# Attention inputs loaded in six pieces a tensor in place of four, and the longest rows of the first loads halved

## The chip, the core and the metric

The kernel runs on one core of a Trainium2 chip. The metric is the device time of one execution in microseconds (us); lower is better. Three executions of the kernel before took 612.52, 612.87 and 614.18 us, so its time is 612.87 us, the median.

## What is computed

Windowed attention, and then a mixture of experts on its output. Cut to what matters:

```python
batch, n_heads, seq, head_dim = (8, 8, 576, 64)
scores = scale * np.matmul(q, k.transpose(0, 1, 3, 2))
rel = pos[:, None] - pos[None, :]
mask = (rel >= 0) & (rel < window)                  # window = 64
scores = np.where(mask, scores, -1000000000.0)
attn = np.exp(scores - np.max(scores, axis=-1, keepdims=True))
attn = attn / (np.sum(attn, axis=-1, keepdims=True) + 1e-09)
attn_out = np.matmul(attn, v)
x = attn_out.transpose(0, 2, 1, 3).reshape(B * S, H * D)   # 4608 x 512
logits = x @ w_gate                                  # 8 experts, 576 tokens each
# tokens are given to experts in the order of their logits, each once, up to a capacity
h = np.maximum(x[mask] @ w1[e], 0.0)
out[mask] = h @ w2[e]
```

## The kernel before

**Stages.** The attention takes the first 147 us or so of the program. Then the tokens are routed, and from about 160 us on eight experts run one after another, with weights streamed in and the results scattered out. The change touches the attention's loads alone.

**The attention.** The queries of one batch are cut into 9 blocks of 64 positions (NB = 9). A step `m` of the loop at L291 works on two blocks, so 8 batches make 36 steps and a new batch begins every four and a half. On TensorE (PE) a step is: the scores of step `m` (L128, tiles Q and K), where a batch begins or goes on also its gate products (L85, tile VT, the values once more, transposed) and their transposes (L95), the product with the values of step `m - 2` (L178, tiles VO and VE), and the transposes of step `m - 1` (L148). ScalarE (ACT) takes the exponentials, VectorE (DVE) the masks, maxima and scalings, GpSimd (POOL) copies values by half a block (VE, L114 and L115). The order is the one that is written; each engine runs its own part in that order and waits on semaphores.

**The loads.** All come from the queue of SyncE (SP), but for two pieces of K at the very start, which ACT issues. For the first two batches, `load_qk`, `load_vt` and `load_v` (L57 to L75) are called with ranges of blocks (L235 to L253); a row is what one of the 128 partitions gets in one DMA, and so it has 1,024 to 5,120 bytes there, cut out of a longer row in memory. From the third batch on `load_all` (L255) loads Q and K in one step and VT and VO in the next, each in four pieces that lie in memory one behind another; a piece has 128 rows of 576 numbers (2,304 bytes) for Q, K and VT, and of 584 (2,336 bytes) for VO. A rest of VO (64 rows of 2,336 bytes, L269) follows. The host writes that order in `lay` (L421). So a batch from the third on takes 17 DMAs. Outputs of the attention go out as stores `xs<-x` (L285) on the same queue, at first held back (HOLD = 14) and let go when the last loads have been issued.

**What limits the queue.** The DMAs of SP share eight semaphores in turn, DMAHW0 to DMAHW7. A DMA waits for the one eight places before it, so at most eight are on their way.

Of the kernel before, what the change touches and what calls it, by code (L numbers as in the profile page):

```python
# [20 lines left out]
B, H, S, D = 8, 8, 576, 64  # L21
NB = S // 64
HP = H // 2
E = 8
WARM = 30
VW = 73
# [2 lines left out]
LOADED = 9 * (B - 3) + 12  # L29


def attention(ctx, tc, c, q, k, v, vt, gate, xs, L, choices, setup, counters, mean, rows, guess):

    nc = tc.nc
    wgbd, wg = gate
# [6 lines left out]
    x = ps.tile([128, 512], FT, name="Tp", bufs=2)  # L42
# [8 lines left out]
    Q, K, VO, VE, VT = {}, {}, {}, {}, {}  # L51
# [2 lines left out]
    PARTS = ((0, 4), (4, NB))  # L54
    BW = HP * 64

    def load_vt(b, i0, i1):  # L57
        if not i0:
            VT[b] = ld.tile([128, NB, HP, 64], FT, name="VT")
        nc.sync.dma_start(VT[b][:, i0:i1].rearrange("p i h s -> p (i h s)"), vt[b, :, BW * i0:BW * i1])  # L60

    def load_qk(b, i0, i1, q2=nc.sync):
        if not i0:
            Q[b] = ld.tile([128, NB, HP, 64], FT, name="Q", bufs=3)
            K[b] = ld.tile([128, NB, HP, 64], FT, name="K", bufs=3)
        for q1, t, x in ((nc.sync, Q, q), (q2, K, k)):
            q1.dma_start(t[b][:, i0:i1].rearrange("p i h s -> p (i h s)"), x[b, :, BW * i0:BW * i1])

    def load_v(b, i0, i1):
        if not i0:  # L70
            VO[b] = ld.tile([128, 5, H, VW], FT, name="VO", bufs=3)
        j0, j1 = i0 // 2, i1 // 2
        nc.sync.dma_start(VO[b][:, j0:j1].rearrange("p j h w -> p (j h w)"), v[b, :, H * VW * j0:H * VW * j1])
        if i1 % 2:
            nc.sync.dma_start(VO[b][0:64, j1].rearrange("p h w -> p (h w)"), v[b, 0:64, H * VW * j1:])  # L75

# [148 lines left out]
    def last():  # L225

        for g, pe in enumerate(P.pop(M - 1)):
# [5 lines left out]
            T.setdefault(M - 1, []).append(pt)  # L233

    load_qk(0, 0, 2, nc.scalar)  # L235
    load_qk(0, 2, 4, nc.scalar)
    nc.sync.dma_start(wgbd, wg)
    counters()
    load_vt(0, *PARTS[0])
    load_qk(0, 4, 6)  # L240
    load_v(0, *PARTS[0])
    load_qk(0, 6, 8)
    load_vt(0, *PARTS[1])
    load_v(0, *PARTS[1])
    load_qk(0, 8, NB)
    load_qk(1, 0, 1)
    load_qk(1, 1, 3)
    load_vt(1, *PARTS[0])
    load_v(1, *PARTS[0])
    load_qk(1, 3, 5)  # L250
    load_qk(1, 5, NB)
# [3 lines left out]
    def load_all(b, part):  # L255
        if not part:
            Q[b] = ld.tile([128, NB, HP, 64], FT, name="Q", bufs=3)
            K[b] = ld.tile([128, NB, HP, 64], FT, name="K", bufs=3)
        else:
            VT[b] = ld.tile([128, NB, HP, 64], FT, name="VT")  # L260
            VO[b] = ld.tile([128, 5, H, VW], FT, name="VO", bufs=3)
        for t, x in ((VT[b], vt), (VO[b][:, 0:4], v)) if part else ((Q[b], q), (K[b], k)):
            t = t.rearrange("p i h w -> p (i h w)").rearrange("p (n x) -> p n x", n=4)
            n = 512 * t.shape[2]
            rows = x[b].rearrange("p x -> (p x)")[0:n].rearrange("(n p x) -> n p x", n=4, p=128)
            for i in range(4):
                nc.sync.dma_start(t[:, i], rows[i])
        if part:
            nc.sync.dma_start(VO[b][0:64, 4].rearrange("p h w -> p (h w)"),  # L269
                              v[b].rearrange("p x -> (p x)")[n:n + 64 * H * VW].rearrange("(p x) -> p x", p=64))  # L270
# [20 lines left out]
    for m in range(M + 1):  # L291
# [65 lines left out]
        for x in loads.get(m, []):  # L357
            load_all(*x)
# [56 lines left out]
def lay(q, k, v, wg):  # L415
    import numpy as np
    def blocks(t):
        t = t.reshape(B, HP, 2, NB, 64, D).transpose(0, 2, 5, 3, 1, 4)
        return np.ascontiguousarray(t).reshape(B, 128, NB * HP * 64)

    va = np.zeros((B, 640, H, VW), np.float32)  # L421
    va[:, :S, :, :D] = v.transpose(0, 2, 1, 3)
    va[:, :S, :, VW - 1] = 1.0
    va = np.ascontiguousarray(va.reshape(B, 5, 128, H * VW).transpose(0, 2, 1, 3)).reshape(B, 128, 5 * H * VW)

    def pieces(t, n):

        t[2:] = t[2:].reshape(B - 2, 128, n, -1).transpose(0, 2, 1, 3).reshape(B - 2, 128, -1)
        return t

    wb = np.zeros((128, HP, 32), np.float32)
    w = wg.reshape(HP, 2, D, E)
    wb[0:64, :, 0:8] = w[:, 0].transpose(1, 0, 2)
    wb[64:128, :, 16:24] = w[:, 1].transpose(1, 0, 2)
    return dict(q=pieces(blocks(q), 4), k=pieces(blocks(k), 4), v=pieces(va, 5), vt=pieces(blocks(v), 4), wg=wb)


NT = 4608
# [976 lines left out]
def body(tc, q, k, v, vt, wg, w1, w2, xs, out):  # L1415
    nc = tc.nc
    with ExitStack() as ctx:
# [6 lines left out]
        with ExitStack() as actx:  # L1424
            attention(actx, tc, c, q, k, v, vt, (wgs, wg), xs, L, lambda j0, j1: rt.choices(j0, j1, 0), rt.setup,
                      rt.counters, (rt.mean, rt.mean_mm, rt.mean_out), rt.rows, rt.guess)
# [49 lines left out]
```

## Time and profile before

| what | us |
|---|---|
| three executions, median | 612.87 (612.52 to 614.18) |
| the profiled execution, its own time | 613.34 |
| its span, first to last instruction | 611.7 |
| PE busy | 588.9 (96%) |
| DVE, ACT, POOL busy | 394.1, 371.8, 198.4 |
| DMA queue q1 (hardware), share of 16 engines' span | 36.0% |

The profile tells of one execution, of 613.34 us, from which 1.6 us lie outside its span. Busy shares are means over stages with different limits; the attention is read by itself below, in stretches of the span. A row of the timeline gives start, length, engine, line, operation, output and input, shape, and in brackets the idle time of the engine before it with what ended that. "issue" there means that the engine waited for nothing that the profile shows. The DMA view of a stretch lists queues with packets, megabytes and the share of 16 engines that their packets took; q1 carries the loads and stores that SP issues, q8 and q14 carry instructions.

### The profile page before, as it was taken

The numbers are of one execution on the slowest core, as the hardware profiler recorded it, in microseconds if no ns is written. First come the engines' busy times: TensorE is split into PE (matmuls) and PEld (weight loads), VectorE is DVE, ScalarE is ACT, GpSimd is POOL, SyncE is SP. The second block draws the span as 40 slices with busy tenths as digits, with TensorE's granted clock in tenths as the row PEclk, the third lists the DMA queues.
The fourth block names the chain that finished last, engine by engine and source line by source line (L and its number), as shares of the span: only waits on it lengthen the run. The fifth ranks groups of instructions, "written<-read, shape, count | busy, mean of one in ns | idle before, by whom it ended". The sixth has DMA issues, their size and how long they took to land.

```text
span 611.7 us, 15537 instructions
## 1 busy us (share of the span) xinstructions
PE 588.9 (96%) x5713; PEld 503.3 (82%) x5713; DVE 394.1 (64%) x1804; ACT 371.8 (61%) x804; POOL 198.4 (32%) x277
## 2 busy tenths in 40 slices
PE   7899999997699999999999999999999999999995
PEld 6677878886499789878988997898899789889984
DVE  6798988888785587369547936773685466705400
ACT  6799989997465477267537735852774375615410
POOL 1334435862431261054117203511530273011011
PEclk9999999998699999999999999999999999999999
DMA  8999999962698699189748938992895689410001
GB/s 314 362 359 358 362 365 376 384 240 89 183 242 173 247 210 243 43 289 229 152 167 229 245 70 270 216 221 97 257 243 111 233 191 330 169 44 34 2 26 53
DMA packets 46104, 128.87 MB, mean 211 GB/s; under 512 B 5824, under 2 KB 6464, under 8 KB 46016
## 3 DMA queue, kind: packets, MB, share of 16 engines
q1 hardware_dynamic: 31744, 79.00, 36.0%
q0 software_dynamic: 13984, 48.25, 34.1%
q8 instruction: 46, 0.75, 0.5%
q10 hardware_dynamic: 288, 0.52, 0.3%
q14 instruction: 42, 0.34, 0.2%
HBM read 82.14 MB, written 18.87 MB: 165 GB/s over the span
## 4 chain that ended last, share of the span: by engine, by line
PE 50%; issue 15%; DMA 5%; POOL 2%; DVE 1%; ACT 1%; POOLq 0%; SPq 0%
PE h L1328 23%; PE o L1372 20%; PE o L1362 4%; DMA st<-w 2%; DMA wl<-st 2%; POOL out L1351 2%; PE tp L1266 1%; DMA xg<-xs,idx 1%; PE rps L685 1%; PE rps L1046 1%; POOL xg L1228 0%; ACT wh L1155 0%; POOLq L1472 0%; POOL wl L1171 0%; DVE hl L1297 0%
## 5 line engine op out<-in xcount | busy, mean ns | idle before, releaser
L1328 PE MATMUL h<-xh,wh 128*128 128x320 f32 (+2 forms) x800 | 159.0, 333 | 0.3 <-DVE hh L1297 0.3
L1328 PEld LDWEIGHTS h<-xh,wh 128*128 128x128 f32 x800 | 124.2, 188 | 5.6 <-ACT sum L1287 0.5
L1351 POOL DMA_INDIRECT out<-ot,idx x40 | 40.1, 1001 | 198.1 <-DVE q L932 82.1
L1372 PE MATMUL o<-wh,hl 128*128 128x512 f32 x256 | 101.3, 396 | 0.0
L1372 PE MATMUL o<-wl,hh 128*128 128x512 f32 x256 | 100.5, 393 | 0.0
L1372 PE MATMUL o<-wh,hh 128*128 128x512 f32 x256 | 100.4, 392 | 0.0
L141 ACT ACTIVATE pe<-st,mx 128x128 f32<-128x128 f32 x288 | 92.0, 394 | 5.4 <-DVE mx L136 5.0
L1328 PE MATMUL h<-xh,wl 128*128 128x256 f32 (+1 forms) x512 | 91.1, 298 | 0.0
L1328 PEld LDWEIGHTS h<-xh,wl 128*128 128x128 f32 x512 | 78.5, 188 | 4.1
L1171 POOL DMA_DIRECT2D wl<-st x51 | 45.9, 1023 | 82.1 <-ACT wl L1169 43.8
L1155 ACT ACTIVATE wh<-st 128x1024 fp32r<-128x1024 f32 x64 | 67.3, 1051 | 4.9 <-DMA st<-w 4.7
L1342 ACT ACTIVATE ot<-o 128x512 f32<-128x512 f32 x32 | 19.2, 599 | 83.7 <-PE o L1372 83.7
L136 DVE CUSTOM_DVE_ANT_0 st<-Sp,mask 128x128 f32<-128x128 f32 x288 | 63.7, 285 | 5.9 <-PE Sp L128 4.5
L1372 PEld LDWEIGHTS o<-wl,hh 128*128 128x128 f32 x256 | 48.1, 188 | 9.5
L1372 PEld LDWEIGHTS o<-wh,hh 128*128 128x128 f32 x256 | 48.1, 188 | 9.4
L1372 PEld LDWEIGHTS o<-wh,hl 128*128 128x128 f32 x256 | 48.1, 188 | 9.3
L1169 ACT ACTIVATE wl<-wh 128x1024 fp32r<-128x1024 f32 x51 | 53.9, 1058 | 1.0
L1289 DVE TENSOR_TENSOR sum<-h,sum 128x256 f32<-128x256 f32 x56 | 23.4, 418 | 40.3 <-ACT sum L1287 39.7
L1292 ACT ACTIVATE hh<-h 128x320 fp32r<-128x320 f32 (+1 forms) x72 | 30.8, 427 | 30.2 <-PE h L1328 30.0
L1228 POOL DMA_INDIRECT xg<-xs,idx x32 | 32.4, 1012 | 42.2 <-DVE eq L970 34.6
L1297 DVE SCALAR_TENSOR_TENSOR hl<-h,hh 128x256 fp32r<-128x256 f32 x72 | 30.0, 417 | 24.1 <-ACT hh L1292 24.0
L153 ACT ACTIVATE pt<-Tp 128x512 f32<-128x512 f32 x70 | 41.1, 587 | 6.7 <-PE Tp L148 6.6
(222 smaller groups left out, 1028.4 us busy)
## 6 DMA issues: line engine op xcount, KB each, us to landing
st<-w SPq DMA_DIRECT2D x59, 512.0 KB, 7.6
wl<-st POOLq DMA_DIRECT2D x51, 512.0 KB, 8.6
xs<-x SPq DMA_DIRECT2D x36, 256.0 KB, 5.8
VO<-v SPq DMA_DIRECT2D x24, 292.0 KB, 6.4
Q<-q SPq DMA_DIRECT2D x24, 288.0 KB, 6.9
K<-k SPq DMA_DIRECT2D x24, 288.0 KB, 6.2
VT<-vt SPq DMA_DIRECT2D x24, 288.0 KB, 5.8
st<-w POOLq DMA_DIRECT2D x5, 512.0 KB, 7.9
```

The costliest lines, as they stand in the source:

```text
L136: nc.vector.tensor_tensor_reduce(st[:, h, :], Sp[h % 2][:, h // 2], mk, scale=-0.125, scalar=3.0e38, op0=OP.add, op1=OP.min, accum_out=mx[ ...
L141: nc.scalar.activation(pe[:, h, :], st[:, h, :], AF.Exp, bias=mx[:, h:h + 1], scale=-1.0)
L153: return pt, lambda: nc.scalar.activation(flat, Tp, AF.Copy)
L1155: nc.scalar.activation(hi, st[i], AF.Copy)
L1169: nc.scalar.activation(lo, hi.bitcast(FT), AF.Copy, scale=-1.0)
L1171: nc.gpsimd.dma_start(lo.bitcast(FT), st[i], accum_op=OP.add)
L1228: nc.gpsimd.indirect_dma_start(out=g[a][0:n], out_offset=None, in_=self.xs, in_offset=IndirectOffsetOnAxis(ap=idx[0:n, a:a + 1], axis=0))
L1292: nc.scalar.activation(hh[:, f, c0:c1], h, AF.Relu)
L1297: nc.vector.scalar_tensor_tensor(t, h[:, a - c0:b - c0], 0.0, hh[:, f, a:b].bitcast(FT), op0=OP.max, op1=OP.subtract)
L1328: nc.tensor.matmul(h[:, 0:w], wv[:, cc, 128 * (f % 2):128 * (f % 2) + 128], x[:, cc, x0:x0 + w], start=(k == 0), stop=(k == 4 * len(terms) ...
L1351: nc.gpsimd.indirect_dma_start(out=self.out[5 * p + a], out_offset=IndirectOffsetOnAxis(ap=idx[0:m, a:a + 1], axis=0), in_=ot[0:m], in_off ...
L1372: nc.tensor.matmul(o, ht[:, f, 128 * a:128 * a + 128], wt[:, 512 * (f % 2):512 * (f % 2) + 512], start=(k == 0), stop=(k == 23))
```

## The change

Three edits. `load_all` cuts Q, K, VT and the first four parts of VO into six pieces in place of four, at multiples of 32 numbers: six of 384 numbers (1,536 bytes a row) for Q, K and VT, five of 384 and one of 416 for VO. `lay` lays the memory out for that. For the first two batches a new helper `halves` cuts a range of more than three blocks in two (rows of 4,096 bytes into two of 2,048, rows of 5,120 into 2,048 and 3,072), and `load_v` loads one part of VO at a time (rows of 4,672 bytes into two of 2,336). No other instruction of the attention is written differently. DMAs of SP grow from 17 to 25 for each batch from the third on, and by five for each of the first two, by 58 in all.

```diff
+def pieces(n):
+
+    cuts = [n * i // (6 * 32) * 32 for i in range(7)]
+    return list(zip(cuts, cuts[1:]))
...
+    def halves(i0, i1):
+        m = (i0 + i1) // 2
+        return [(i0, m), (m, i1)] if i1 - i0 > 3 else [(i0, i1)]
...
-        nc.sync.dma_start(VT[b][:, i0:i1].rearrange("p i h s -> p (i h s)"), vt[b, :, BW * i0:BW * i1])
+        for i, j in halves(i0, i1):
+            nc.sync.dma_start(VT[b][:, i:j].rearrange("p i h s -> p (i h s)"), vt[b, :, BW * i:BW * j])
...
-        for q1, t, x in ((nc.sync, Q, q), (q2, K, k)):
-            q1.dma_start(t[b][:, i0:i1].rearrange("p i h s -> p (i h s)"), x[b, :, BW * i0:BW * i1])
+        for i, j in halves(i0, i1):
+            for q1, t, x in ((nc.sync, Q, q), (q2, K, k)):
+                q1.dma_start(t[b][:, i:j].rearrange("p i h s -> p (i h s)"), x[b, :, BW * i:BW * j])
...
-        j0, j1 = i0 // 2, i1 // 2
-        nc.sync.dma_start(VO[b][:, j0:j1].rearrange("p j h w -> p (j h w)"), v[b, :, H * VW * j0:H * VW * j1])
+        j1 = i1 // 2
+        for j in range(i0 // 2, j1):
+            nc.sync.dma_start(VO[b][:, j].rearrange("p h w -> p (h w)"), v[b, :, H * VW * j:H * VW * (j + 1)])
...
-            t = t.rearrange("p i h w -> p (i h w)").rearrange("p (n x) -> p n x", n=4)
-            n = 512 * t.shape[2]
-            rows = x[b].rearrange("p x -> (p x)")[0:n].rearrange("(n p x) -> n p x", n=4, p=128)
-            for i in range(4):
-                nc.sync.dma_start(t[:, i], rows[i])
+            t = t.rearrange("p i h w -> p (i h w)")
+            rows = x[b].rearrange("p x -> (p x)")
+            n = 128 * t.shape[1]
+            for i, j in pieces(t.shape[1]):
+                nc.sync.dma_start(t[:, i:j], rows[128 * i:128 * j].rearrange("(p x) -> p x", p=128))
...
-    def pieces(t, n):
+    def apart(t, n):
...
-        t[2:] = t[2:].reshape(B - 2, 128, n, -1).transpose(0, 2, 1, 3).reshape(B - 2, 128, -1)
+        cuts = pieces(n) + [(n, t.shape[2])] * (n < t.shape[2])
+        t[2:] = np.concatenate([t[2:, :, i:j].reshape(B - 2, -1) for i, j in cuts], 1).reshape(B - 2, 128, -1)
```

The orders below give line, operation, output and input, the output's shape, and the semaphores waited for. First SP's queue at the start of the program, the loads of batch 0, before:

```order
L60 DMA VT_163<-vt 128x1024
L67 DMA Q_152<-q 128x512
L67 DMA K_153<-k 128x512
L73 DMA VO_167<-v 128x1168 [waits DMAHW0_49]
L67 DMA Q_152<-q 128x512 [waits DMAHW1_49]
L67 DMA K_153<-k 128x512 [waits DMAHW2_49]
L60 DMA VT_163<-vt 128x1280 [waits DMAHW3_49]
L73 DMA VO_167<-v 128x1168 [waits DMAHW4_49]
L75 DMA VO_167<-v 64x584 [waits DMAHW5_49]
```

And now:

```order
L71 DMA VT_163<-vt 128x512 x2
L79 DMA Q_152<-q 128x512
L79 DMA K_153<-k 128x512 [waits DMAHW0_49]
L86 DMA VO_168<-v 128x584 [waits DMAHW1_49]
L86 DMA VO_168<-v 128x584 [waits DMAHW2_49]
L79 DMA Q_152<-q 128x512 [waits DMAHW3_49]
L79 DMA K_153<-k 128x512 [waits DMAHW4_49]
L71 DMA VT_163<-vt 128x512 [waits DMAHW5_49]
L71 DMA VT_163<-vt 128x768 [waits DMAHW6_49]
L86 DMA VO_168<-v 128x584 [waits DMAHW7_49]
```

The order of the tensors is the same; the pieces are smaller, and the waits for a semaphore begin one DMA earlier (the first is K's and no longer VO's).

Second, SP's queue where the third batch is loaded (Q_400, K_401 and VT_511 are its tiles), before, from the last pieces of K on:

```order
L267 DMA K_401<-k 128x576 [waits DMAHW4_49]
L267 DMA VT_511<-vt 128x576 [waits DMAHW5_49,PE_49]
L267 DMA VT_511<-vt 128x576 [waits DMAHW6_49]
L267 DMA VT_511<-vt 128x576 [waits DMAHW7_49]
L267 DMA VT_511<-vt 128x576 [waits DMAHW0_49]
L267 DMA VO_512<-v 128x584 [waits DMAHW1_49]
```

And now:

```order
L280 DMA K_411<-k 128x384 [waits DMAHW2_49]
L280 DMA VT_525<-vt 128x384 [waits DMAHW3_49,PE_49]
L280 DMA VT_525<-vt 128x384 [waits DMAHW4_49]
L280 DMA VT_525<-vt 128x384 [waits DMAHW5_49]
L280 DMA VT_525<-vt 128x384 [waits DMAHW6_49]
L280 DMA VT_525<-vt 128x384 [waits DMAHW7_49]
L280 DMA VT_525<-vt 128x384 [waits DMAHW0_49]
L280 DMA VO_526<-v 128x384 [waits DMAHW1_49]
```

Six DMAs of VT stand where four stood. Each still waits for the DMA eight places before it, and the first still waits for PE, which has to be done with the tile of two batches before.

Third, PE's two gate products of the fourth batch (step 13), before:

```order
L85 MATMUL Tp<-VT,wgs 32x256 [waits DMAHW7_49,DMAHW6_49,Activation_49]
L85 MATMUL Tp<-VT,wgs 32x256 x3
L85 MATMUL Tp<-VT,wgs 32x320 [waits DMAHW1_49,DMAHW0_49,Activation_49]
L85 MATMUL Tp<-VT,wgs 32x320 x3
```

And now:

```order
L98 MATMUL Tp<-VT,wgs 32x256 [waits DMAHW5_49,DMAHW6_49,DMAHW4_49,Activation_49]
L98 MATMUL Tp<-VT,wgs 32x256 x3
L98 MATMUL Tp<-VT,wgs 32x320 [waits DMAHW1_49,DMAHW7_49,DMAHW0_49,Activation_49]
L98 MATMUL Tp<-VT,wgs 32x320 x3
```

The products stand where they stood; each waits for three pieces of VT in place of two.

## Rows read from the trace of the kernel before

**Rows 1.** The page: busy time; granted clock and DMA in 40 slices; the instruction queue.

```profile
PE 588.9 (96%) x5713; PEld 503.3 (82%) x5713; DVE 394.1 (64%) x1804; ACT 371.8 (61%) x804; POOL 198.4 (32%) x277
...
PEclk9999999998699999999999999999999999999999
DMA  8999999962698699189748938992895689410001
...
q8 instruction: 46, 0.75, 0.5%
```

**Rows 2.** Stretches (start:end; busy us and count by engine; granted clock, DMA share, GB/s).

```profile
20.00:142.00 122.00, 119.71 (x2464) 96.93 (x2460) 108.27 (x750) 113.09 (x338) 65.49 (x121) 1.00 0.96 343
```

**Rows 3.** Waits of PE up to 190 us: the only one for a DMA.

```profile
PE Sp L128 <- DMA Q<-q: 0.4, 1, 0.4
```

**Rows 4.** Timeline of PE, 16 to 19 us.

```profile
16.12 0.73 PE L85 MATMUL Tp<-VT,wgs 128*32 128x320 f32 x3
18.24 0.73 PE L85 MATMUL Tp<-VT,wgs 128*32 128x320 f32 x5 [1.39 <-issue]
```

**Rows 5.** Timeline of PE, 86.4 to 88.9 us.

```profile
86.54 1.10 PE L128 MATMUL Sp<-K,Q 64*64 64x128 f32 x32
88.87 0.28 PE L178 MATMUL Op<-VE,pt 128*64 128x73 f32 x1 [1.23 <-DVE mx L136]
```

**Rows 6.** Timeline of DVE, 86.9 to 87.8 us.

```profile
87.06 0.68 DVE L218 TENSOR_TENSOR x<-Op,r 128x512 f32<-128x512 f32 x1
```

**Rows 7.** DMA view, 15.5 to 17 us.

```profile
DMA packets 403, 0.42 MB, mean 282 GB/s; under 512 B 46, under 2 KB 362, under 8 KB 402
...
q8 instruction: 1, 0.02, 5.4%
```

**Rows 8.** DMA view, 86 to 87.5 us (issues: KB each, median us to landing).

```profile
q8 instruction: 1, 0.02, 4.6%
issues: line engine op xcount, KB each, median us to landing
Q<-q SPq DMA_DIRECT2D x2, 288.0 KB, 5.9
```

**Rows 9.** DMA view, 17 to 87.5 us: the instruction queue.

```profile
q8 instruction: 11, 0.18, 1.1%
```

**Rows 10.** Stretches from the start to the end of each of the two gaps.

```profile
0.00:18.20 18.20, 13.70 (x219) 10.59 (x220) 12.93 (x102) 10.71 (x30) 2.85 (x12) 1.00 0.93 315
0.00:88.80 88.80, 82.04 (x1607) 65.41 (x1607) 74.73 (x535) 75.66 (x222) 31.80 (x61) 1.00 1.01 352
```

**Rows 11.** DMA view, 133.7 to 140.2 us, when the loads are done.

```profile
q8 instruction: 1, 0.02, 1.0%
...
xs<-x SPq DMA_DIRECT2D x3, 256.0 KB, 2.0
```

**Rows 12.** DMA view, 23.5 to 27 us: mostly rows of 4,096 and 5,120 bytes.

```profile
DMA packets 357, 1.45 MB, mean 413 GB/s; under 512 B 40, under 2 KB 40, under 8 KB 357
```

**Rows 13.** DMA view, 46.2 to 50.5 us: rows of 2,304 bytes.

```profile
DMA packets 811, 1.68 MB, mean 390 GB/s; under 512 B 89, under 2 KB 89, under 8 KB 810
```

**Rows 14.** DMA view, 40.7 to 44.9 us: the four pieces of the third batch's VO.

```profile
DMA packets 600, 1.23 MB, mean 294 GB/s; under 512 B 74, under 2 KB 74, under 8 KB 599
```

**Rows 15.** DMA view, 48.3 to 48.6 us: the last piece of the fourth batch's VT.

```profile
VT<-vt SPq DMA_DIRECT2D x1, 288.0 KB, 7.4
```

**Rows 16.** Timeline of PE, 56.5 to 59 us: its gate products.

```profile
57.11 1.18 PE L85 MATMUL Tp<-VT,wgs 128*32 128x256 f32 x16
```

**Rows 17.** DMA view, 111.04 to 111.2 us: the last piece of the eighth batch's VT.

```profile
VT<-vt SPq DMA_DIRECT2D x1, 288.0 KB, 5.8
```

**Rows 18.** Timeline of PE, 125 to 127 us: its gate products.

```profile
125.41 1.29 PE L85 MATMUL Tp<-VT,wgs 128*32 128x256 f32 x16
```

**Rows 19.** Timeline of SP, 14 to 19.7 us.

```profile
17.33 0.43 SPq L67 DMA_DIRECT2D Q<-q  x1
17.81 0.43 SPq L67 DMA_DIRECT2D K<-k  x1
18.28 0.43 SPq L67 DMA_DIRECT2D Q<-q  x1
```

More of the change, by code (lines that the diff above doesn't have):

```diff
@@ L434, in lay @@
     wb[64:128, :, 16:24] = w[:, 1].transpose(1, 0, 2)
-    return dict(q=pieces(blocks(q), 4), k=pieces(blocks(k), 4), v=pieces(va, 5), vt=pieces(blocks(v), 4), wg=wb)
+    n = NB * HP * 64
+    return dict(q=apart(blocks(q), n), k=apart(blocks(k), n), v=apart(va, 4 * H * VW), vt=apart(blocks(v), n), wg=wb)
 NT = 4608
```

## The prediction

> **What bounds the kernel now.** The page comes first [rows 1]: PE is busy for 96% of the span, at the upper of its two clock levels (2.4 GHz) until the attention is over, and in the first eight slices or so the 16 DMA engines are full too. So both could set the pace of the attention, and the next view has to tell which. From 20 to 142 us PE is busy for 119.71 of 122 us, while ACT has 113.09 and DVE 108.27 [rows 2]. PE's waits confirm it: one wait for a DMA stands there, 0.4 us at the very start, for the first piece of Q [rows 3], which the change leaves as it is. The loads run ahead of PE. Faster or slower loads by themselves therefore change nothing, as long as they stay ahead.
>
> What is left to win is PE's idle time between those products, and two gaps hold nearly all of it: 1.39 us before 18.24, in the middle of a gate product, with "issue" as its cause [rows 4], and 1.23 us before 88.87 [rows 5]. The second is put down to DVE, but DVE's last result that this product needs, the scaled x that empties Op, was done at 87.06 + 0.68 = 87.74 [rows 6], and PE's work before ended at 86.54 + 1.10 = 87.64. So 0.10 us of that wait is DVE's, and 1.13 us are not explained by it.
>
> I read both gaps as PE without instructions. The queue of instructions, q8, delivered one packet shortly before each gap ended: one between 15.5 and 17 us [rows 7], one between 86 and 87.5 [rows 8]. On the page 46 packets serve 2 x 5713 rows of PE, 248 a packet [rows 1]. Between the two gaps q8 has 11 packets [rows 9] and PE 2 x 1607 - 219 - 220 = 2775 rows [rows 10]: 252 rows a packet, so both gaps fall at the same place of a packet's run, as they would if PE had used up what it held. The packets are not slow: by their share of 16 engines they took 0.054 x 16 x 1.5 = 1.3 us and 1.1 us, and 1.0 us when nearly nothing else ran [rows 7, 8, 11]. They came late. The data of the same moment needed 5.9 us from issue to landing [rows 8], and 2.0 us when the loads were over [rows 11]; up to eight DMAs lie ahead of whatever comes.
>
> **The change, part by part.** *Six pieces in place of four.* The queue still holds eight DMAs. Eight of 288 KB (2.36 MB) are 6.0 us of work at 390 GB/s [rows 13]; eight of 192 KB (1.57 MB) are 4.3 us at the 369 GB/s worked out below. A late refill would come up to 1.7 us earlier, and the second gap needs 1.13. *Halved rows at the start.* The eight DMAs from the first VT on were 512, 256, 256, 584, 256, 256, 640 and 584 KB, 3.4 MB; now 256, 256, 256, 256, 292, 292, 256 and 256, 2.2 MB. At 413 GB/s [rows 12] that is 8.3 against 5.3 us, 3.0 less, where the first gap needs 1.39. So I take out both: 1.39 + 1.13 = 2.52 us. Bounds: 0, if refills do not wait behind data, to 2.62 with DVE's tenth. I take nearly the upper end because the two packets stand where the reading wants them. PE goes on without a pause after each, and ACT and DVE have 9 and 14 us of room in the 122 [rows 2], so the gain reaches the end.
>
> *The loads themselves.* No row shows 1,536 bytes in a row. The nearest show 413 GB/s with rows of 1.45 MB / 317 = 4,574 bytes on average [rows 12], 390 with 2,304 [rows 13], and 282 in a stretch mostly of 1,024 bytes, cut out of a longer row in memory [rows 7]. Per engine a row of 4,574 takes 16 x 4,574 / 413 = 177 ns, one of 2,304 takes 94.5; the straight line through both gives 66.6 ns for 1,536, or 369 GB/s. That is an estimate; the ends are 390 and 282. I go by the line, since the new rows lie one behind another as those of 2,304 do, and those of 1,024 do not. The first batches' halved ranges (5.80 MB) go from 413 to 390 at worst: 14.0 to 14.9 us, 0.8 more.
>
> The place where this can matter is the fourth batch's VT, the load with the least room. Its last piece was issued at about 48.35 and took 7.4 us [rows 15], so it landed at about 55.8; the second of the two gate products begins halfway through the row at 57.11 [rows 16], at 57.7. Room: 1.9 us, and 0.5 once the first gap is gone. Up to there 8.27 MB come in the new pieces (the third batch, and Q, K and VT of the fourth): 21.2 us at 390, 22.4 at 369, 1.2 more. With the 0.8 above the loads are 2.0 us late. Against it, the third batch's VO with its rows of 2,336 bytes ran at 294 GB/s [rows 14]: 1.20 MB took 4.1 us, 1.0 more than at 390, and its new rows are like the others. I count that 1.0 as won back, so VT is 1.0 late and PE waits 0.5 us. Bounds: 0 and, at 369 with nothing won back, 1.5. Later batches have more room: the eighth's VT landed at about 111.05 + 5.8 = 116.85 [rows 17] and is wanted at 125.41 [rows 18], 123.4 after the gain; 27.2 MB up to there cost 4.0 + 0.8 us, which 6.5 us of room covers. The stores behind them are small work: three of them stand in the 6.5 us after 133.7 [rows 11].
>
> *SP and the added waits.* SP issues a DMA every 0.48 us when nothing holds it [rows 19], 192 KB / 0.48 us = 410 GB/s, above every rate taken here; 58 more of them cost nothing while the engines have seven others to work on. If that cover went, SP would be the bound at 25 x 0.48 = 12 us a batch, against 17 us that PE needs for four and a half steps (18 steps lie between the gate products of the fourth and the eighth batch, 125.41 - 57.11 = 68.3 us [rows 16, 18]). A gate product waits for three pieces in place of two; semaphores that are already up hold PE for nothing (the row at 16.12 has no bracket [rows 4]).
>
> **Sum.** 613.34 (the profiled execution) - 1.39 - 1.13 + 0.5 = 611.3 us. That execution is 0.5 above the median, and the three others lie 0.8 on either side of it, which is the spread that I give the sum: 610.5 to 612.1.
>
> **Rivals.** *The refills do not wait behind data.* Then neither gap goes, or one by chance: 613.3, or 613.34 - 1.2 = 612.1 with one gone. For it speaks that other refills under the same full queue caused no gap: ten of the 11 up to the second. Against it, both gaps come with a full queue and at the same place of a packet.
>
> The Trainium skill speaks for this rival (DMA: Bandwidth & Descriptors, Queues, rings and completion order): an engine goes round its queues packet by packet, so a refill would wait for a packet or two and not for eight DMAs. No row shows a refill's request, so the trace can't settle that; by this rule the time would be the rival's.
>
> *The loads win instead.* The odd rows of VO cost in each batch what they cost in the third, and nothing is late: no wait of 0.5, 610.8, and 610.0 at the lower end of the spread.
>
> *The loads fall behind*, the case on the other side. With less on its way, a hiccup of SP or a late landing leaves the engines without work, and the short rows run nearer to 282 than to 390. The end is then set by the gate products of the late batches. Half way, 325 GB/s, the 27.2 MB up to the eighth VT take 83.7 in place of 69.8 us; with the first batches' 0.8 it is 14.7 late, the room without gaps is 6.0, and PE waits 8.7: 610.8 + 8.7 = 619.5. It decides from about 345 GB/s down, where the wait passes 3.9 us and the time 614.7. For it speaks that short rows are the slowest in the trace; against it, that 2,304 has lost only 6% to rows twice as long.
>
> The Trainium skill speaks for this one too (DMA: Bandwidth & Descriptors, Rules for kernel authors): DMAs of a megabyte or more for full bandwidth, small ones put together. The trace agrees in the direction (390 against 413 GB/s); how much a further third costs no row shows.
>
> **How the numbers follow.** The sum has 0.50. It lies near the bound at which a measurement of this kernel can tell a gain, 0.3% or 1.84 us below the median, 611.03, so 0.25 of it counts as faster and 0.25 as within. Loads that win have 0.15, all faster. Refills that don't wait have 0.21, all within 0.3%. Loads that fall behind have 0.14, slower. Faster 0.40, same 0.46, slower 0.14. The range takes in the first three, from 610.0 to 613.3 and half a microsecond of spread above, 613.8; the fourth stays outside.
>
> **What would show it.** Right: no gap of PE over 0.5 us with "issue" or an unexplained cause between 15 and 131 us; data landing in about 4.3 us in place of 6; DMA near 370 GB/s in the loads of the third batch and later; a wait of PE or ACT around the fourth batch's gate products of 0 to 1.5 us. The first step is wrong if the gaps stay while landing gets shorter, or if new ones stand elsewhere at the same place of a packet. The second is wrong if the loads end later than 126 us, or PE's rows show waits for VT from the fifth batch on. The whole is wrong if the attention ends no earlier although both gaps are gone: then ACT or DVE held it.

## The result, and the profile after

The changed kernel takes 620.18 us (median of five executions, 616.95 to 622.96) against 612.87 for the kernel before in the same session (612.38 to 614.18). The ratio is 1.0114, with a 95% interval of 1.0071 to 1.0157: slower by 1.1%. The prediction was 611.3 us in a range of 610.0 to 613.8, so it was wrong, and it was wrong about the sign. The time is the one of the third rival, loads that fall behind (619.5 us).

The profiled execution took 621.96 us. Lines of its page: busy time of PE; granted clock and DMA share in 40 slices; the chain that ended last; the DMAs of the attention with their median time to land.

```profile
PE 590.9 (95%) x5713; PEld 505.0 (81%) x5713; DVE 393.8 (63%) x1804; ACT 372.6 (60%) x804; POOL 198.7 (32%) x277
...
PEclk9998998999699999999999999999999999999998
DMA  8999999998399589479928956892897599510001
...
PE 56%; DMA 19%; issue 16%; SPq 3%; POOL 3%; DVE 1%; ACT 0%; POOLq 0%; DVEq 0%
...
xs<-x SPq DMA_DIRECT2D x36, 256.0 KB, 4.6
Q<-q SPq DMA_DIRECT2D x36, 192.0 KB, 4.8
K<-k SPq DMA_DIRECT2D x36, 192.0 KB, 4.6
VT<-vt SPq DMA_DIRECT2D x36, 192.0 KB, 4.9
VO<-v SPq DMA_DIRECT2D x30, 192.0 KB, 4.9
```

The same lines of the page before, as far as they were not shown:

```profile
PE 50%; issue 15%; DMA 5%; POOL 2%; DVE 1%; ACT 1%; POOLq 0%; SPq 0%
...
xs<-x SPq DMA_DIRECT2D x36, 256.0 KB, 5.8
VO<-v SPq DMA_DIRECT2D x24, 292.0 KB, 6.4
Q<-q SPq DMA_DIRECT2D x24, 288.0 KB, 6.9
K<-k SPq DMA_DIRECT2D x24, 288.0 KB, 6.2
VT<-vt SPq DMA_DIRECT2D x24, 288.0 KB, 5.8
```

PE does the same 5713 products. What is new is DMA in the chain, 19% of the span where it was 5%: the attention now waits for loads. A DMA lands sooner than before, in 4.8 us where it was 6.3 (means of the four medians), but it carries a third less, and the DMA engines stay busy for one slice longer. The granted clock drops to 0.8 in two slices of the attention, where [rows 1] has no such dip before its end.

Stretches of the profile after (start:end; busy us and count by engine; granted clock, DMA share, GB/s). The first answers to [rows 2].

```profile
20.00:142.00 122.00, 112.26 (x2231) 89.90 (x2232) 97.74 (x681) 102.30 (x303) 55.95 (x105) 0.97 0.96 316
...
32.00:60.00 28.00, 24.24 (x468) 19.25 (x464) 20.71 (x146) 21.76 (x64) 7.54 (x13) 0.94 0.95 291
60.00:90.00 30.00, 28.90 (x607) 23.04 (x596) 26.29 (x186) 26.66 (x80) 12.98 (x23) 1.00 0.96 307
...
50.00:60.00 10.00, 9.84 (x174) 7.79 (x176) 7.89 (x53) 7.29 (x21) 2.85 (x5) 0.84 0.92 277
...
100.00:110.00 10.00, 8.13 (x125) 6.52 (x117) 6.87 (x47) 6.13 (x19) 5.30 (x8) 0.83 0.99 339
```

And two stretches of the profile before, in which all the traffic is loads in pieces and stores:

```profile
32.00:60.00 28.00, 27.36 (x556) 21.62 (x554) 24.53 (x173) 25.69 (x76) 9.78 (x17) 1.00 1.05 358
60.00:90.00 30.00, 28.51 (x599) 23.36 (x597) 27.10 (x188) 27.81 (x83) 12.78 (x22) 1.00 1.02 363
```

The loads run at 291 and 307 GB/s where they ran at 358 and 363, and the engines, which were full, have 4 to 5% of idle time. That is less than the 15 to 19% that the rate lost: the packets also took longer for their bytes (q1 from 60 to 90 us: 94.5% of the 16 engines for 9.10 MB, before 100.8% for 10.78). The last load is issued at 133.58 us and lands at 137.9; before, at 114.64 and 120.8. SP's timeline after:

```profile
133.58 0.48 SPq L282 DMA_DIRECT2D VO<-v  x1
```

**Where PE lost it.** DVE's waits up to 160 us, those for a DMA (sum, times, longest), and then PE's:

```profile
DVE x L231 <- DMA xs<-x: 6.0, 3, 2.9
...
DVE VO L114 <- DMA VO<-v: 3.8, 1, 3.8
```

```profile
PE Tp L161 <- DVE VO L114: 3.8, 2, 3.1
PE Op L191 <- DVE x L231: 1.3, 1, 1.3
PE Op L191 <- DVE oh L591: 1.2, 1, 1.2
...
PE Sp L141 <- DMA K<-k: 0.8, 1, 0.8
```

In order of time, DVE's timeline and PE's:

```profile
49.27 0.29 DVE L114 COPY VO<-Tp 128x128 f32<-128x128 f32 x1 [3.82 <-DMA VO<-v]
...
101.49 0.69 DVE L231 TENSOR_TENSOR x<-Op,r 128x512 f32<-128x512 f32 x1 [2.38 <-DMA xs<-x]
...
119.33 0.69 DVE L231 TENSOR_TENSOR x<-Op,r 128x512 f32<-128x512 f32 x1 [2.86 <-DMA xs<-x]
```

```profile
15.99 0.74 PE L98 MATMUL Tp<-VT,wgs 128*32 128x320 f32 x8
...
49.62 0.92 PE L161 MATMUL Tp<-ident,pe 128*128 128x128 f32 x4 [3.12 <-DVE VO L114]
...
92.30 0.25 PE L191 MATMUL Op<-VE,pt 128*64 128x73 f32 x1 [0.32 <-POOL VE L128]
...
102.33 0.25 PE L191 MATMUL Op<-VE,pt 128*64 128x73 f32 x1 [1.22 <-DVE oh L591]
...
120.08 0.28 PE L191 MATMUL Op<-VO,pt 128*64 128x73 f32 x1 [1.25 <-DVE x L231]
```

Two resources are late, and neither is the VT that the prediction watched. At 49.27 DVE's copy of the gate columns has to write into the third batch's VO, whose pieces are still landing; before, this copy ran at 47.26 and waited only for PE, since the last of that VO had landed at 45.6 (issued at 38.39, 7.2 us to landing):

```profile
47.26 0.29 DVE L101 COPY VO<-Tp 128x128 f32<-128x128 f32 x1 [0.64 <-PE Tp L95]
```

At 101.49 and 119.33 DVE wants a buffer for the scaled values x, and its 18 buffers are all still waiting to be stored: the stores stand in SP's queue behind loads that are late. The row at 102.33 names DVE's oh (L591), but that row of DVE comes straight behind the x that waited.

The start of PE's scores, step by step against the kernel before, makes the account. Gains: 1.2 us over the first steps (2.1 at the step of the first gap, of which 1.2 are lost again at the next step, where PE waits 0.8 us for K) and 0.9 at the step of the second gap. Losses: 3.4 us at 49, 1.2 right behind it, 1.0 at 62 (a wait of 0.74 for ACT in PE's gate products), 2.7 and 0.9 at 102 and behind it, 1.9 at 120; 11.1 in all. With a remainder of 0.3 the attention ends 9.3 us later. PE's waits at these places are 3.12 + 0.74 + 1.22 + 1.25 = 6.3 us of the 11.1. The other 4.7 are a difference and no row. Behind the first and the third of these waits lie the two stretches with a granted clock of 0.84 and 0.83, which by that clock account for at most 1.6 and 1.7 us of it (0.16 and 0.17 of 10 us); the remaining 1.4 or so are not explained.

### The profile page after: what moved, and what is told of

Its sections match the earlier page's. It is cut to its first block, busy times and chain, and to the rows that moved or that the text cites. A ratio compares the mean times of both kernels' runs of the same rounds, so it can differ in the third digit from the quotient of the medians.

```text
span 620.3 us, 15624 instructions
## 1 busy us (share of the span) xinstructions
PE 590.9 (95%) x5713; PEld 505.0 (81%) x5713; DVE 393.8 (63%) x1804; ACT 372.6 (60%) x804; POOL 198.7 (32%) x277
## 4 chain that ended last, share of the span: by engine, by line
PE 56%; DMA 19%; issue 16%; SPq 3%; POOL 3%; DVE 1%; ACT 0%; POOLq 0%; DVEq 0%
PE h L1343 24%; PE o L1387 20%; DMA VO<-v 6%; DMA VT<-vt 4%; DMA K<-k 4%; PE o L1377 4%; DMA wl<-st 3%; SPq L280 2%; PE Tp L161 2%; POOL out L1366 2%; PE tp L1281 1%; PE Sp L141 1%; PE Op L191 1%; PE rps L700 1%; DMA Q<-q 1%
## 5 line engine op out<-in xcount | busy, mean ns | idle before, releaser
L161 PE MATMUL Tp<-ident,pe 128*128 128x128 f32 x288 | 41.1, 284 | 5.5 <-DVE VO L114 3.8
```

The lines of the kernel that those rows point to most:

```text
L161: nc.tensor.transpose(Tp[:, 128 * h:128 * h + 128], pe[:, h, :], c["ident"])
```

## The experiments

Theories: **places**: SP has eight DMAs in flight at most, so what matters is how many bytes these eight hold; **SP's time**: 25 issues a batch leave SP no time to catch up; **rows**: rows of 1,536 bytes cost the engines too much; **start**: the halves at the beginning delay all that follows. Places and SP's time were one theory at first ("count" or "issue" in the expectations), until the last pair split it.

| kernel | DMAs a batch | KB each | shortest row of a piece, bytes | GB/s, 60 to 90 us | last load lands, us | attention against before, us | time to before (95%) |
|---|---|---|---|---|---|---|---|
| before | 17 | 288 | 2,304 | 363 | 120.8 | 0 | 1 |
| the change | 25 | 192 | 1,536 | 307 | 137.9 | +9.3 | 1.0114 (1.0071 to 1.0157) |
| halves_only | 17 | 288 | 2,304 | 376 | 121.5 | -1.3 | 0.998 (0.9958 to 1.0002) |
| six_only | 25 | 192 | 1,536 | 316 | 134.7 | +6.5 | 1.0096 (1.0072 to 1.0119) |
| short_rows_17_dmas | 17 | 288 | 1,152 | 347 | 126.5 | +0.2 | 1.002 (1.0003 to 1.0037) |
| long_rows_25_dmas | 25 | 144, 288 | 2,304 | 259 | 155.8 | +27.4 | 1.0461 (1.0431 to 1.049) |
| tiny_25 | 17 and 8 tiny | 288, 1 | 2,304 | 306 | 137.5 | +10.8 | 1.0147 (1.011 to 1.0184) |
| sp_busy_17 | 17 | 288 | 2,304 | 360 | 124.9 | +0.4 | 0.9984 (0.9959 to 1.0009) |
| five_pieces | 21 | 224, 240 | 1,792 | 357 | 125.9 | -1.1 | 0.9996 (0.9974 to 1.0018) |
| five_qk_four_v | 19 | 224 to 304 | 1,792 | 369 | 123.2 | -0.8 | 0.9997 (0.9979 to 1.0014) |
| three_pieces | 13 | 384 | 3,072 | 384 | 120.7 | +1.3 | 1.0033 (1.0013 to 1.0052) |
| six_stores_pool | 25, stores on POOL | 192 | 1,536 | 335 | 130.5 | +3.7 | 1.0122 (1.0084 to 1.0161) |

"Attention against before" is the start of the last step's scores in the profiled execution against 139.43 us before.

### Which part of the change: halves_only, six_only

halves_only keeps the first half of the diff (`halves`, and VO by single blocks) and takes back the second:

```diff
-            for i, j in pieces(t.shape[1]):
-                nc.sync.dma_start(t[:, i:j], rows[128 * i:128 * j].rearrange("(p x) -> p x", p=128))
+            for i in range(4):
+                nc.sync.dma_start(t[:, i], rows[i])
```

> The first two batches' loads cut in two as in the change, the later batches in four pieces as before. Theory of the issue (17 DMAs a batch leave SP time to catch up, 25 of 192 KB don't): the later batches run as before, PE's gap of 1.39 us at step 4 goes and leaves a wait of about 0.3 for the first batch's K, so 611.7 us (610.9 to 612.6). Theory of the rows (1,536-byte rows cost the engines too much): the same, 611.7. Theory of the start (the halves end the second batch's loads 2.5 us later and the later loads never make it up): most of the 7.3 us are there, 618 to 621.

six_only keeps the second half and loads the first two batches as before.

> Six pieces from the third batch on, the first two batches as before. Issue and rows alike: waits for the third batch's VO and for values buffers come back, 619 to 622 us. Theory of the start: 612.5 to 614.

Measured: 612.06 us for the halves, ratio 0.998, and 619.04 us for the six pieces, ratio 1.0096. The halves gain about 1.2 us, though the interval just reaches 1, and the whole loss is in the six pieces. The start theory falls. In six_only DVE waits 4.8 us for one values buffer; the third batch's VO is on time there, so which of the two late resources is hit first depends on how the start went.

### Rows or count: short_rows_17_dmas, long_rows_25_dmas

The kernel before with each of its pieces laid out in memory as two runs of 1,152 bytes a partition, still one DMA:

```diff
-            t = t.rearrange("p i h w -> p (i h w)").rearrange("p (n x) -> p n x", n=4)
-            n = 512 * t.shape[2]
-            rows = x[b].rearrange("p x -> (p x)")[0:n].rearrange("(n p x) -> n p x", n=4, p=128)
+            t = t.rearrange("p i h w -> p (i h w)").rearrange("p (n r x) -> p n r x", n=4, r=2)
+            n = 1024 * t.shape[3]
+            rows = x[b].rearrange("p x -> (p x)")[0:n].rearrange("(n r p x) -> n p r x", n=4, r=2, p=128)
```

> The kernel before with each piece of 288 KB still one DMA, but its memory laid out in rows of 1,152 bytes, two to a partition, so 17 DMAs a batch with rows shorter than the change's. Issue: SP issues as before, so the loads end near 121 us and the time is 612 to 614 us. Rows: the engines pay twice the number of rows, more than in the change, so 620 us or more (up to 630), with waits for VO and values buffers.

And with the rows of before, but two of the four pieces in two DMAs of 64 partitions:

```diff
             for i in range(4):
-                nc.sync.dma_start(t[:, i], rows[i])
+                for p0, p1 in ((0, 64), (64, 128)) if i % 2 == 0 else ((0, 128),):
+                    nc.sync.dma_start(t[p0:p1, i], rows[i, p0:p1])
```

> The kernel before with rows of 2,304 and 2,336 bytes, but the first and the third piece of every tensor in two DMAs of 64 partitions each: 25 DMAs a batch as in the change, no row shorter than before. Issue: SP falls behind as in the change, loads end after 130 us, 618 to 622 us. Rows: as before, 612 to 614 us.

Rows shorter than the change's cost 0.2% (614.2 us). The stretch of 60 to 90 us of short_rows_17_dmas:

```profile
60.00:90.00 30.00, 29.21 (x607) 24.02 (x604) 27.10 (x189) 27.64 (x83) 12.81 (x22) 1.00 1.07 347
```

347 GB/s, and after its first piece of Q PE waits for no load. The prediction's line through two row lengths gives 16 x 1,152 / 52.6 ns = 350 GB/s for this length, so its price of a short row was right, and the row length can't be what took the change to 307. The rows theory falls.

The other kernel went to 640.32 us, far over what either theory said. Its DMA view, 60 to 90 us:

```profile
DMA packets 3960, 7.77 MB, mean 259 GB/s; under 512 B 626, under 2 KB 626, under 8 KB 3952
...
q1 hardware_dynamic: 3952, 7.67, 98.4%
```

The engines are full here at 259 GB/s, while the change leaves them idle time at 307. Each byte was dearer in the engines in this kernel, so it does not tell count from rows; why half the partitions cost so much is open.

### Count alone: tiny_25

A DMA of 1 KB behind the second and one behind the fourth piece of each tensor, in the kernel before:

```diff
                 nc.sync.dma_start(t[:, i], rows[i])
+                if i % 2:
+                    nc.sync.dma_start(spare[:, SPN[0] % 8], q[0, 0:16, 0:16])
+                    SPN[0] += 1
```

> The kernel before, with eight more DMAs of 1 KB a batch (16 rows of 64 bytes into a spare tile that nobody reads), two after the pieces of each tensor: 25 DMAs a batch as in the change, no row and no piece of the loads changed. Count (each DMA takes SP's issue time and one of the eight places in flight, so with eight small ones some 5.4 of the eight hold pieces, 1.6 MB as in the change): loads at 300 to 340 GB/s, ending at 128 to 138 us, 615 to 621 us. Rows: as before, 612 to 614 us.

622.96 us, 1.0147: 8 KB more a batch cost as much as the whole change. Two lines of its DMA view, 60 to 90 us:

```profile
DMA packets 4926, 9.18 MB, mean 306 GB/s; under 512 B 966, under 2 KB 966, under 8 KB 4918
...
spare<-q SPq DMA_DIRECT2D x14, 1.0 KB, 4.9
```

306 GB/s, the rate of the change, with the rows of before. A DMA of 1 KB needs 4.9 us to land, as long as the pieces beside it, and holds its place all that time. Its bytes are not what costs: its rows of 64 bytes took 11 ns each in the trace, 0.5% of the engines' time. And here too the engines' packets took longer for their bytes (92.8% of the 16 engines for 9.09 MB), so longer packets need no shorter rows.

### Places or SP's time: sp_busy_17

The same places in the program, but a register load in place of the small DMA (the loaded value steers nothing):

```diff
+                if i % 2:
+                    nc.sync.value_load(zi[0:1, 0:1], min_val=0, max_val=E - 1)
```

> The kernel before with eight more register loads a batch on SP (a zero from SBUF, whose value nobody uses), where tiny_25 has its small DMAs: by the register loads that the program already has on SP, 0.41 us and 0.18 for what follows each, so 4.7 us of SP's time a batch, more than eight issues take (3.6 us), and no place in flight. SP's time as the cause: late like tiny_25, 617 to 624 us, loads ending after 128 us. The eight places as the cause: as before, 612 to 614 us, loads at 355 to 365 GB/s.

612.2 us, 0.9984. The register loads took 0.47 us each with what follows them, 3.8 us a batch, about what eight issues take and less than was expected. From 60 to 90 us SP's own instructions fill 24.0 us, in the change 23.5, in tiny_25 22.8, before 15.7. The stretch of 60 to 90 us:

```profile
60.00:90.00 30.00, 29.32 (x622) 24.23 (x618) 27.23 (x191) 27.89 (x85) 13.16 (x23) 1.00 1.01 360
```

With as much of SP's time gone as in tiny_25, but no place, the loads keep their rate and the time does not change. So SP's time alone is not the cause; it takes the places. (The direct trial, another number of places with everything else as before, was not made.) SP's time is not free either: over 32 to 120 us this kernel moves 347 GB/s against 367 before, and its last load lands 4 us later; that stays inside the room.

### How much must the eight hold: five_pieces, three_pieces, five_qk_four_v

The number of pieces of the change set to five, to three, and to five for Q and K with four for VT and VO:

```diff
-    cuts = [n * i // (6 * 32) * 32 for i in range(7)]
+    cuts = [n * i // (5 * 32) * 32 for i in range(6)]
```

> The change with five pieces in place of six (21 DMAs a batch, rows of 1,792 bytes and over, 230 KB a DMA). If eight places in flight set the rate, it lies between 307 GB/s at 192 KB and 365 at 288 KB, near 335, the loads end at 127 to 130 us, and the time lies between: 612 to 616 us. If six pieces fail by something of their own (SP without time to catch up), five are as good as four: 611 to 612.5.

> The change with three pieces in place of six (13 DMAs a batch, rows of 3,072 bytes, 384 KB a DMA). Eight places then hold 3 MB: loads at 370 to 395 GB/s ending before 120 us, landing 7.5 to 8.5 us; PE's refills wait 6 to 8 us behind them, so several gaps of 1 to 3 us at refills: 612 to 620 us. If refills don't wait behind the data: 610 to 612 us.

> Halves in the first two batches, then Q and K in five pieces, VT and VO in four (19 DMAs a batch, 230 and 288 KB). With eight places setting the rate: 350 to 360 GB/s, between four and five pieces, no wait for a load or a values buffer, both of PE's long refill gaps gone, so 1 to 2 us under the kernel before: 611 to 612.3 us. If the refills came back it is as before, 612.5 to 613.5.

Five pieces: 612.88 us, as before; three: 615.47, slower by 0.3%; the mix: 613.24, as before, where 611 to 612.3 was expected. Their stretches of 60 to 90 us, one kernel each, five, three and the mix:

```profile
60.00:90.00 30.00, 29.34 (x623) 24.17 (x614) 27.62 (x194) 28.00 (x85) 13.02 (x23) 1.00 1.04 357
```

```profile
60.00:90.00 30.00, 28.43 (x579) 23.15 (x579) 26.20 (x181) 26.55 (x79) 12.79 (x22) 1.00 1.03 384
```

```profile
60.00:90.00 30.00, 29.30 (x606) 24.12 (x605) 27.48 (x193) 27.62 (x83) 12.85 (x22) 1.00 1.04 369
```

The bytes in eight places divided by the time to land give these rates to within about 7%: 1.57 MB / 4.8 us = 328 GB/s for six pieces (307 measured; the 45 DMAs of these 30 us, at some 5.0 us each, fill 7.4 of the eight places on average), 1.89 MB / 5.2 us = 363 for five (357), 2.36 MB / 6.3 us = 375 for four (363), 3.15 MB / 7.7 us = 409 for three (384). With 230 KB and more the rate grows slowly and the time to land takes up the rest; with 192 KB the rate falls. This says how size, time and rate hang together, and not why a DMA of 192 KB still needs 4.8 us while the engines have idle time; no run shows that. The 357 of five pieces are also nearer to the other theory's "as good as four" than to the 335 that were expected of the places; it is sp_busy_17 that speaks against SP's time, and not this run. The loss in time begins between 347 and 316 GB/s (60 to 90 us).

Three pieces have the best rate and lose on the other side. PE's waits from 20 to 130 us in that kernel:

```profile
PE Op L191 <- issue: 1.9, 2, 1.0
```

Two waits of 1 us with no cause but "issue", before 50.19 and 64.54 us, as at [rows 4]. The stretches up to them:

```profile
0.00:50.18 50.18, 44.73 (x849) 35.55 (x850) 40.59 (x299) 40.67 (x119) 15.63 (x34) 1.00 0.98 338
0.00:64.53 64.53, 57.97 (x1101) 45.55 (x1101) 51.43 (x373) 52.41 (x153) 20.72 (x44) 1.00 0.99 344
```

PE has 849 + 850 = 1699 and 2202 rows behind it there, against 219 + 220 = 439 at the first gap of [rows 10]: 1260 and 1763 more, 5.0 and 7.0 times 252. So these are refills too, and with 3 MB ahead of them they come late in places where they came in time before.

### Is it SP's queue or the engines: six_stores_pool

```diff
-        nc.sync.dma_start(xs[128 * m:128 * m + 128], x.rearrange("p h d -> p (h d)"))
+        nc.gpsimd.dma_start(xs[128 * m:128 * m + 128], x.rearrange("p h d -> p (h d)"))
```

> The change with the stores of values issued by POOL's queue in place of SP's. If SP's queue (its issues and its eight places) is what the change ran short of: the loads have it to themselves, end before 130 us, no wait for values buffers, 611 to 615 us; POOL pays 36 issues of about 1 us. If the engines themselves are short (rows), the total of loads and stores moves no faster: 618 to 623 us.

620.11 us, so no gain, and in the range expected if the engines are short, though part of the other expectation came true: DVE no longer waits for a values buffer, and the attention ends 3.7 us late in place of 9.3. What tells the two apart is the rate. The DMA view from 60 to 90 us:

```profile
DMA packets 6880, 10.05 MB, mean 335 GB/s; under 512 B 800, under 2 KB 6553, under 8 KB 6873
...
q1 hardware_dynamic: 6633, 9.17, 94.1%
q0 software_dynamic: 240, 0.79, 6.7%
```

The engines carry 335 GB/s when a second queue brings work, while SP's own queue still gives 9.17 MB in 30 us, 306 GB/s. So the queue and not the engines holds the change at 307. The loads have gained only the stores' share, and VT and VO are still waited for (2.3 and 1.5 us). The rest of the loss, 2.6 us in the profiled span, stands behind PE's last product; what causes it there was not tried.

## Why the prediction was wrong

**The step that failed** is in "Six pieces in place of four": "Eight of 288 KB (2.36 MB) are 6.0 us of work at 390 GB/s [rows 13]; eight of 192 KB (1.57 MB) are 4.3 us at the 369 GB/s worked out below." The rate was taken from the length of a row, and the time to land followed from it. It goes the other way: the time to land fell only to 4.8 us, and eight places of 192 KB then give 328 GB/s, 307 measured. With that the sum's term for late loads, + 0.5, fails: the losses of the change sum to 11.1 us. The prediction reckoned that seven others in flight cover SP ("cost nothing while the engines have seven others to work on") without asking whether seven of 192 KB are still enough. tiny_25 and sp_busy_17 show the difference: SP's time alone costs nothing that reaches the end, with the place it does.

**The two refill gaps** were rightly put down to refills: in all twelve kernels, every wait of PE over 0.15 us in the attention with "issue" as its cause stands a whole number of times 252 rows, to within 12, from the first gap (0, 2, 4, 5, 7, 8, 14 or 15 times). What takes them away was read rightly for the first at most. In the change PE's first gate product runs in one piece (the row at 15.99, against [rows 4]). That the halves do it is made likely by all kernels together, one profile each, at the same place each time, between the third and the fourth of the eight products at line 85 of before:

| first two batches | gap there, us |
|---|---|
| as before (before, six_only, short_rows_17_dmas, long_rows_25_dmas, sp_busy_17, tiny_25) | 1.39, 2.24, 1.42, 2.24, 1.70, 0 |
| halved (the change, halves_only, five_pieces, five_qk_four_v, three_pieces, six_stores_pool) | 0, 0.41, 0.88, 0.87, 0, 0 |

The mean is 1.50 against 0.36; the size was taken as certain and is partly chance (tiny_25 has the loads of before and no gap). PE's timeline of halves_only shows a gap that is shorter and in the same place:

```profile
15.84 0.73 PE L92 MATMUL Tp<-VT,wgs 128*32 128x320 f32 x3
16.98 0.73 PE L92 MATMUL Tp<-VT,wgs 128*32 128x320 f32 x5 [0.41 <-issue]
```

The second gap did not go because of the six pieces. The wait of 1.23 us of [rows 5] is 0.32 in the change, but at this place it is 0.20 to 0.43 in every other kernel too, also where pieces of 288 KB lie ahead; halves_only and then sp_busy_17:

```profile
87.60 0.25 PE L185 MATMUL Op<-VE,pt 128*64 128x73 f32 x1 [0.30 <-POOL VE L122]
```

```profile
89.29 0.25 PE L178 MATMUL Op<-VE,pt 128*64 128x73 f32 x1 [0.31 <-POOL VE L115]
```

It stood in the one profiled execution of the kernel before, and no run shows the 1.13 us of the sum as the worth of smaller pieces.

The rival that refills don't wait behind data is weakened by the table and by three_pieces; it is not ruled out, since most refills behind a full queue left no gap. By the Trainium skill (DMA: Bandwidth & Descriptors, Queues, rings and completion order) an engine serves its queues in turn, packet by packet, so that a refill would pass after a packet or two of another queue. The means of 1.50 and 0.36 us go with the bytes ahead and speak against that here, though no row shows when a refill was asked for. Of the 2.52 us of the sum, halves_only ends the attention 1.3 earlier and five_pieces at most 2.0 (steps 22 to 26); in both, 0.9 of it comes at the second gap, as in sp_busy_17, and so by chance.

**The loads.** The line through the row lengths was good (350 against 347 at 1,152 bytes). That the bounds of 282 and 390 hold the measured 291 and 307 is luck: they were bounds for the length of the rows, and that was not the cause. The sign "wrong if the loads end later than 126 us" came true with 137.9.

**The place with the least room** was sought in VT alone. The third batch's VO had 1.7 us (landed at 45.6, copied at 47.26). At 291 in place of 358 GB/s the third batch's 4.9 MB take 16.8 in place of 13.6 us, some 3 more, which is over that room. "The stores behind them are small work" failed too: they are small for the engines, but in SP's queue they wait behind every late load, and x has 18 buffers.

**The rival on the other side** had the right direction and the right point, and its time of 619.5 us is luck: by its own sum the measured 307 GB/s give 88.6 us in place of 69.8 for the 27.2 MB, so 624.4 us. It said that the loads decide "from about 345 GB/s down": in the table, kernels at 347 and above end the attention within 1.3 us of the kernel before, the one at 335 in all 3.7 late, those at 316 and below 6.5 or more. Its place, the late gate products, was not where it showed, and its chance of 0.14 was too low. What it named in passing, "with less on its way", was the cause. The Trainium skill (DMA: Bandwidth & Descriptors, Rules for kernel authors), large DMAs and small ones put together, pointed the same way, and the runs agree: 307, 357, 363 and 384 GB/s at 192, 230, 288 and 384 KB.

**The clock** was not in the sum. After two of PE's long waits, those before 49.62 and 102.33, the granted clock of the stretch falls to 0.84 and 0.83, which costs at most some 3.3 of the 11.1 us; after the one before 120.08 it stays at 1.00.

No version here beats the kernel before by more than the measurement: halves_only has 0.998 (0.9958 to 1.0002).

## What to carry to other kernels

Where a queue has a fixed number of DMAs in flight, a smaller piece buys a shorter wait for what stands behind it and pays with rate: divide the bytes that the places hold by the time to land, and compare it with the rate that the consumer needs before cutting. A DMA of 1 KB costs a place like one of 288 KB. Look for the least room among all that shares the queue, the stores and their buffers included, and not only at the load that the next product names.

## What was not expected

A DMA of 1 KB took 4.9 us to land beside pieces of 288 KB. With half of the pieces in DMAs of 64 partitions the engines were full at 259 GB/s, where DMAs of 128 with the same rows ran at 363. An issue of SP, 0.33 to 0.48 us as a rule, took over 1 us sixteen times in the first 150 us of the change, at most 1.9, and four times before. From 53.5 to 55 us, around one of them, the DMA view has a packet of the instruction queue. SP's timeline there and the queue's line:

```profile
53.58 1.66 SPq L280 DMA_DIRECT2D VT<-vt  x1
```

```profile
q8 instruction: 1, 0.02, 5.4%
```

Whether the one holds the other, and what these issues add to the loss, was not tried.
